# Layer 1 of a fused expert kernel: remainders in one run of row tiles, and no sums carried from one two pairs to the next

## The chip, the cores and the metric

The kernel runs on one core of a Trainium2 chip. Its time is the device time of one launch in microseconds. Besides that there is a profile of one execution, with a page of summary tables and a trace of every instruction on TensorE (PE, with its weight loads PEld), VectorE (DVE), ScalarE (ACT), GpSimd (POOL) and the DMA queues (SP is the queue of SyncE). Times in the trace count from the start of the span.

## The reference, cut to what matters

Two blocks follow each other: a recurrent attention cell (mLSTM) over 4 batches, 8 heads and 768 positions, and a mixture of 8 experts to which each of the 3072 rows is sent by a hash of its token number. The change concerns the second block and the passage to it.

```python
# attention: y (B, H, S, 40), one state update per position   ... cut ...
x = attn_out.transpose(0, 2, 1, 3).reshape(3072, 320)

expert_idx = token_ids * 2654435761 % 8
for e in range(8):
    mask = expert_idx == e
    xe = x[mask]                          # about 384 rows, 320 columns
    h = np.maximum(xe @ w1[e], 0.0)       # w1[e]: 320 x 1024   (layer 1)
    out[mask] = h @ w2[e]                 # w2[e]: 1024 x 320   (layer 2)
```

All of it is float32.

## The kernel before

The rows of an expert are gathered into 416 columns (384 and a remainder of 32), turned so that the 320 features lie along partitions: two blocks of 128 (`xT[:, 0]`, `xT[:, 1]`) and a block of 64 features, which is present twice, in partitions 0 to 63 (`lo`) and 64 to 127 (`up`). Layer 1 makes eight blocks of 128 hidden features. Expert 0 uses the plain `layer1`. Experts 1 to 7 use `layer1_pairs`: the two blocks of 128 features, two neighbouring blocks of hidden features and two halves of the columns (`c0`, `c1`, 208 each) form a product of 2x2 blocks, done with seven block products in place of eight by a scheme of sums of the Strassen kind. `wsums` holds the four sums of weights (made by POOL), `xsums` the four sums of x (made by DVE). The 64 features left over, the remainder, are added by matmuls of half height: `lo` and `up` are row tiles of PE which run at the same time and write to different PSUM banks. Each `both` is one block product for two pairs of hidden blocks, two float32 matmuls, which are four instructions in the trace. Two passes (`q`) make the eight hidden blocks.

```python
def sums_of_x(xT):
    b = [[xT[:, k, c * CH : (c + 1) * CH] for c in range(2)] for k in range(3)]
    ...                                   # t1, t2, t3, t4: four DVE sums
    nc.vector.tensor_tensor(dx[P // 2 :], b[2][0][P // 2 :], b[2][1][P // 2 :], op=ALU.subtract)
    return t1, t2, t3, t4, dx

def both(q, dst, x, y, start, stop):
    for i in range(2):
        nc.tensor.matmul(dst[:, i, :], lhsT=x(2 * q + i), rhs=y, ...)

def last(dst1, x1, dst2, x2, q, stop2):   # the remainder: two row tiles side by side
    for i in range(2):
        for d, r, x in ((dst1, lo, x1), (dst2, up, x2)):
            nc.tensor.matmul(d[:, i, :], lhsT=w1c[r, 2 * q + i, :], rhs=x, start=False, ...)

prev = None
for q in range(NQ + 1):                   # NQ = 2
    cur = None
    if q < NQ:
        A, B, Y = (PSUM banks)
        p1, u2, v = (SBUF tiles, bufs=2, 2, 1)
        cur = q, B, Y, p1, u2
        both(q, A, blk(0, 0), xT[:, 0, c0], True, True)
        nc.scalar.copy(p1[:], A[:])                                        # L1067
        both(q, B, of(s2), t2[:], True, True)
        nc.vector.tensor_tensor(u2[:], B[:], p1[:], op=ALU.add)            # L1069
        both(q, Y, of(s3), t3[:], True, False)
        between(2 * q)
    if prev:                              # second half of the pairs before
        pq, pB, pY, pp1, pu2 = prev
        both(pq, pY, blk(1, 1), t4[:], False, False)
        both(pq, pB, of(s4), xT[:, 1, c1], False, False)
    if cur and prev:
        both(q, B, of(s1), t1[:], False, True)
        nc.vector.tensor_tensor(v[:], B[:], p1[:], op=ALU.add)             # L1078
    if cur:
        last(A, xT[lo, 2, c0], Y, xT[up, 2, c1], q, True)
    if prev:
        last(pB, xT[lo, 2, c1], pY, dx[up], pq, True)
    if cur and not prev:
        both(q, B, of(s1), t1[:], False, True)
        nc.vector.tensor_tensor(v[:], B[:], p1[:], op=ALU.add)             # L1085
    if cur:
        nc.vector.tensor_tensor(hv[:, 1, ..., c1], Y[:], v[:], op=ALU.add) # L1087
    if prev:
        h0, h1 = (hv[:, i, ...] for i in range(2))
        nc.vector.tensor_tensor(h1[:, :, c0], pY[:], pu2[:], op=ALU.add)   # L1090
        nc.scalar.activation(h1, h1, AF.Relu)                              # L1091
        nc.vector.tensor_tensor(h0[:, :, c1], pB[:], pp1[:], op=ALU.add)   # L1092
        nc.scalar.activation(h0[:, :, c1], h0[:, :, c1], AF.Relu)          # L1093
    if cur:
        both(q, A, blk(1, 0), xT[:, 1, c0], False, True)
        nc.scalar.activation(hv[:, 0, ..., c0], A[:], AF.Relu)             # L1096
        between(2 * q + 1)
    prev = cur
```

`between` takes the next of the following expert's `turns`: three tiles of 128 rows and a remainder. A turn is three transposes on PE and a copy out of PSUM (tile 0 and 2 on DVE, tile 1 and the remainder on ACT). Layer 2 (`layer2_pair`) begins with one plain product and makes the others from sums in the same way; it calls `after(j)` at three points. In the loop over the experts:

```python
def one(fp):
    if ahead and (e > 0 or fp != 0 or len(ahead) < 4):
        ahead.pop(0)()
def after(j):
    if j == (e == 0) and e + 1 < E:
        xss[e + 1] = sums_of_x(xTs[e + 1])
    one(j)
    ...
```

The passage from the attention block to expert 0: the last rows are gathered, transposed and copied (L904); `rows_by_table` adds the last 256 rows by a matmul with a table of ones; `spin0(n)` issues n idle products of 416 columns (L890); DVE adds both parts (L911). Then `sums_of_w2` of expert 0 (four POOL sums, L1105) and `fetch(1)`, the gathers of expert 1's rows, follow on POOL in this order.

Of the kernel before, what the change touches and what calls it, by code (L numbers as in the profile page):

```python
# [17 lines left out]
P = 128  # L18
# [4 lines left out]
def kernel(  # L23
# [105 lines left out]
    with tc.tile_pool(name="gates", bufs=1) as gp, \  # L129
# [757 lines left out]
        def spin0(n):  # L887
            idle = ps.tile([P, CAP], F32, name="idle", tag="tr", bufs=4)
            for _ in range(n):
                nc.tensor.matmul(idle[:], lhsT=ident[:], rhs=W[0][0][:, 0, :CAP], start=True, stop=True)  # L890
# [6 lines left out]
        for i, j in enumerate((NJ, *range(NJ))):  # L897
            n = RM if j == NJ else P
            tp = ps.tile([P, DB, P], F32, name="tp0", tag="tr", bufs=4)
            for db in range(2):  # L900
                nc.tensor.transpose(tp[:, db, :n], xg0[:n, j, db * P : (db + 1) * P], ident[:n, :n])  # L901
            nc.scalar.copy(xg0[:n, j, Dm:], xg0[:n, j, 2 * P : Dm])
            nc.tensor.transpose(tp[:, 2, :n], xg0[:n, j, 2 * P :], ident[:n, :n])
            nc.scalar.copy(xT0[:, :, j * P : j * P + n], tp[:, :, :n])  # L904
            if i < DB:
                rows_by_table(1, i)
            if i == DB - 1:
                spin0(1)
        spin0(2)
        for db in range(DB):  # L910
            nc.vector.tensor_tensor(xT0[:, db, :], xT0[:, db, :], om[db][:, :CAP], op=ALU.add)  # L911

# [102 lines left out]
    def sums_of_x(xT):  # L1015

        b = [[xT[:, k, c * CH : (c + 1) * CH] for c in range(2)] for k in range(3)]
        t1, t2, t3, t4, dx = (xp.tile([P, CH], F32, name=f"xs{i}", bufs=1) for i in range(1, 6))
        nc.vector.tensor_tensor(t1[:], b[0][1], b[0][0], op=ALU.subtract)
        nc.vector.tensor_tensor(t2[:], b[1][1], t1[:], op=ALU.subtract)  # L1020
        nc.vector.tensor_tensor(t3[:], b[1][1], b[0][1], op=ALU.subtract)
        nc.vector.tensor_tensor(dx[P // 2 :], b[2][0][P // 2 :], b[2][1][P // 2 :], op=ALU.subtract)
        nc.vector.tensor_tensor(t4[:], b[1][0], t2[:], op=ALU.subtract)
        return t1, t2, t3, t4, dx

    def layer1_pairs(w, wsums, xT, xsums, h, between):

        w1t, w1c, _ = w  # L1030
        s1, s2, s3, s4 = wsums
        t1, t2, t3, t4, dx = xsums
        lo, up = slice(0, P // 2), slice(P // 2, P)
        c0, c1 = slice(0, CH), slice(CH, CAP)
        hv = h.rearrange("p (x i) c -> p i x c", i=2)

        def both(q, dst, x, y, start, stop):
            for i in range(2):
                nc.tensor.matmul(  # L1039
                    dst[:, i, :], lhsT=x(2 * q + i), rhs=y, start=(start and i == 0), stop=stop,  # L1040
                    skip_group_check=True,
                )

        def blk(k, i):
            return lambda fp: w1t[:, k, (2 * fp + i) * P : (2 * fp + i + 1) * P]

        def of(s):
            return lambda fp: s[:, fp]

        def last(dst1, x1, dst2, x2, q, stop2):  # L1050
            for i in range(2):
                for d, r, x in ((dst1, lo, x1), (dst2, up, x2)):
                    nc.tensor.matmul(
                        d[:, i, :], lhsT=w1c[r, 2 * q + i, :], rhs=x, start=False, stop=(r == lo or stop2),
                        skip_group_check=True,
                    )

        NQ = FB // 4
        prev = None
        for q in range(NQ + 1):  # L1060
            cur = None
            if q < NQ:
                A, B, Y = (mps.tile([P, 2, CH], F32, name=f"m{i}", tag="bank") for i in "aby")
                p1, u2, v = (xp.tile([P, 2, CH], F32, name=f"l{i}", bufs=2 - i // 2) for i in range(3))
                cur = q, B, Y, p1, u2
                both(q, A, blk(0, 0), xT[:, 0, c0], True, True)
                nc.scalar.copy(p1[:], A[:])  # L1067
                both(q, B, of(s2), t2[:], True, True)
                nc.vector.tensor_tensor(u2[:], B[:], p1[:], op=ALU.add)  # L1069
                both(q, Y, of(s3), t3[:], True, False)  # L1070
                between(2 * q)
            if prev:
                pq, pB, pY, pp1, pu2 = prev
                both(pq, pY, blk(1, 1), t4[:], False, False)
                both(pq, pB, of(s4), xT[:, 1, c1], False, False)
            if cur and prev:
                both(q, B, of(s1), t1[:], False, True)
                nc.vector.tensor_tensor(v[:], B[:], p1[:], op=ALU.add)  # L1078
            if cur:
                last(A, xT[lo, 2, c0], Y, xT[up, 2, c1], q, True)  # L1080
            if prev:
                last(pB, xT[lo, 2, c1], pY, dx[up], pq, True)
            if cur and not prev:
                both(q, B, of(s1), t1[:], False, True)
                nc.vector.tensor_tensor(v[:], B[:], p1[:], op=ALU.add)  # L1085
            if cur:
                nc.vector.tensor_tensor(hv[:, 1, 2 * q : 2 * q + 2, c1], Y[:], v[:], op=ALU.add)  # L1087
            if prev:
                h0, h1 = (hv[:, i, 2 * pq : 2 * pq + 2, :] for i in range(2))
                nc.vector.tensor_tensor(h1[:, :, c0], pY[:], pu2[:], op=ALU.add)  # L1090
                nc.scalar.activation(h1, h1, AF.Relu)  # L1091
                nc.vector.tensor_tensor(h0[:, :, c1], pB[:], pp1[:], op=ALU.add)  # L1092
                nc.scalar.activation(h0[:, :, c1], h0[:, :, c1], AF.Relu)  # L1093
            if cur:
                both(q, A, blk(1, 0), xT[:, 1, c0], False, True)
                nc.scalar.activation(hv[:, 0, 2 * q : 2 * q + 2, c0], A[:], AF.Relu)  # L1096
                between(2 * q + 1)
            prev = cur

    def sums_of_w2(w2t):  # L1100

# [64 lines left out]
    with tc.manual_schedule():  # L1166
        xgs, xTs, remT, hrem = {}, {0: xT0}, {}, {}

        def fetch(e):
            if e % EG == 0 or e == 1:  # L1170
                xgs[-1 - e // EG] = xp.tile([P, DB * P], F32, name="xr")
            xgs[e] = xp.tile([P, NJ, DB * P], F32, name="xg", bufs=3)
            for j in range(NJ):
                gather(xgs[e][:, j, :Dm], cols_of(g_idx, e * NJ)(j))
            if e % EG == 0 or e == 1:
                gather(xgs[-1 - e // EG][:, :Dm], cols_of(g_idx, NR + e // EG)(0))
# [16 lines left out]
        def rest(g):  # L1193
# [6 lines left out]
                    )  # L1200
            scatter(zp, cols_of(s_idx, NR + g)(0), True)

        sums = sums_of_w2(W[0][2])
        fetch(1)


        for piece in weight_slices(1):
# [2 lines left out]
        for e in range(E):  # L1210
            g, i = e // EG, e % EG
            if e + 2 < E:
                fetch(e + 2)
            if e > 0:
                sums = sums_of_w2(W[e][2])
            h = xp.tile([P, FB, CAP], F32, name="h", bufs=1)
            if i == 0:
                hrem[g] = xp.tile([P, EG, FB, RM], F32, name="hrem")
            ahead = turns(e + 1) if e + 1 < E else []

            def one(fp):
                if ahead and (e > 0 or fp != 0 or len(ahead) < 4):
                    ahead.pop(0)()

            def after(j):
                if j == (e == 0) and e + 1 < E:
                    xss[e + 1] = sums_of_x(xTs[e + 1])
                one(j)
                if j == 0 and i == EG - 1:
                    rest(g)  # L1230

            if e + 1 < E:
                wnext, pieces = sums_of_w1(W[e + 1][0])
            if e == 0:
                layer1(W[e], xTs[e], h, CAP, one)
            else:
                layer1_pairs(W[e], wsums, xTs[e], xss[e], h, one)
            for piece in pieces:
                piece()
            pieces = []  # L1240
            nc.scalar.copy(hrem[g][:, i], h[:, :, NM:])
            layer2_pair(W[e], sums, h, cols_of(s_idx, e * NJ), after)
            wsums = wnext

            if e + 2 < E:
                for j in range(NJ):
                    nc.scalar.copy(xgs[e + 2][:, j, Dm:], xgs[e + 2][:, j, 2 * P : Dm])
                if (e + 2) % EG == 0:
                    xr = xgs[-1 - (e + 2) // EG]
                    nc.scalar.copy(xr[:, Dm:], xr[:, 2 * P : Dm])  # L1250
            if e + 3 < E:
                slices = weight_slices(e + 3)
                if e == 0:
                    slices[1:1] = weight_slices(2)
                for piece in slices:
                    piece()
# [51 lines left out]
```

## Time and profile before

| what | value |
|---|---|
| time, median of 3 | 405.84 us (404.99 to 406.05) |
| span of the profiled execution | 402.9 us |
| granted TensorE clock, mean | 0.983 |
| DVE busy | 221.3 us (55%) |
| ACT busy | 148.8 us (37%) |
| POOL busy | 201.3 us (50%) |
| `ma`, `mb`, `my` full-height matmuls, 128x208, each | 339 to 346 ns |
| row tiles of the remainder, 64x208, each | 336 ns |

[...]matmuls that follow each other overlap. What a matmul costs is read from the distance between two starts. The engine lines of the timeline give the start, the duration, the engine, the line of the program, what is written and read, and in brackets how long the engine sat idle before and which instruction ended it. The attention block fills about the first 155 us, expert 0 begins at 167.8, expert 1 at 196.9, and the last product of expert 7 ends at about 394.

### The profile page before, as it was taken

To read this page: it belongs to the slowest core of one execution; us is meant where nothing else is said; L and a number is where in the kernel's file an instruction comes from. 1 tells how busy PE (TensorE), PEld (TensorE's weight loads), DVE (VectorE), ACT (ScalarE), POOL (GpSimd) and SP (SyncE) were. 2 spreads that over 40 slices of the span, in tenths; PEclk is the share of its full clock that TensorE was granted. 3 is DMA by queue.
4 is the path that set the end of the run, shared out by engine and by line. 5 is a ranking of instruction groups with operands and counts; after the bars stand their busy time and mean duration, and the time that the engine had idled before them with its cause. 6 is when DMAs were issued, how large, how long until landed. Compare 5 with 4: busy or idle time off the path is not lost. (4 is left out here: it accounts for less than half of the span.)

```text
span 402.9 us, 8802 instructions
## 1 busy us (share of the span) xinstructions
PE 378.4 (94%) x3397; PEld 311.6 (77%) x3397; DVE 221.3 (55%) x537; ACT 148.8 (37%) x290; POOL 201.3 (50%) x253
## 2 busy tenths in 40 slices
PE   8789979999999997899999999999999999999991
PEld 8668868877877774457898978978979989889780
DVE  8657557778797984133447356462455463453500
ACT  6335785575676541222132231141131141321310
POOL 6653103324535634881295593871692874807011
PEclk9969999999999999999999999999999999999996
DMA  7588846977767513835938245244244200000000
GB/s 150 111 174 190 205 107 152 242 197 176 151 149 182 132 65 126 285 83 164 333 129 272 75 130 171 83 130 152 83 142 142 78 16 33 2 15 34 0 17 36
DMA packets 96616, 51.53 MB, mean 128 GB/s; under 512 B 68455, under 2 KB 90604, under 8 KB 96572
## 3 DMA queue, kind: packets, MB, share of 16 engines
q1 hardware_dynamic: 90956, 39.29, 37.8%
q0 software_dynamic: 2528, 8.24, 6.2%
q10 hardware_dynamic: 3088, 3.41, 2.8%
q8 instruction: 28, 0.46, 0.5%
q14 instruction: 16, 0.13, 0.1%
HBM read 42.02 MB, written 8.65 MB: 126 GB/s over the span
## 5 line engine op out<-in xcount | busy, mean ns | idle before, releaser
L929 POOL DMA_INDIRECT out_dram<-zo,s_idx x26 | 26.9, 1035 | 91.5 <-DVE zo L1159 53.2
L476 POOL TENSOR_TENSOR x<-x,den 128x320 f32<-128x320 f32 x21 | 15.1, 723 | 48.8 <-DVE den L474 27.4
L387 DVE TENSOR_TENSOR w<-sp,w 128x512 f32<-128x512 f32 x48 | 30.9, 686 | 12.6 <-PE sp L379 12.0
L1121 PE MATMUL zp<-w2t,h 128*128 128x320 f32 x128 | 36.5, 438 | 0.0
L379 PE MATMUL sp<-qT,kT 64*128 64x128 f32 x384 | 29.4, 291 | 2.7 <-ACT qT L316 1.5
L379 PEld LDWEIGHTS sp<-qT,kT 64*128 64x128 f32 x384 | 24.6, 193 | 9.3 <-issue 4.6
L1121 PEld LDWEIGHTS zp<-w2t,h 128*128 128x128 f32 x128 | 23.2, 190 | 11.1 <-issue 1.8
L1091 ACT ACTIVATE h<-h 128x832 f32<-128x832 f32 x14 | 12.6, 898 | 47.6 <-DVE h L1090 47.6
L342 ACT ACTIVATE w<-ab 128x512 f32<-128x512 f32 x48 | 26.6, 608 | 7.5 <-PE ab L338 7.5
L1131 PE MATMUL zp<-t,s 128*128 128x160 f32 x192 | 27.5, 299 | 0.6 <-DVE s L1116 0.6
L437 PE MATMUL ht<-w,v 128*64 128x128 f32 x384 | 27.1, 285 | 0.0
L1131 PEld LDWEIGHTS zp<-t,s 128*128 128x128 f32 x192 | 26.5, 190 | 0.8 <-POOL ws L1013 0.8
L1105 POOL TENSOR_TENSOR t<-w2t 128x640 f32<-128x640 f32 x16 | 24.8, 1548 | 1.7 <-PE tp L901 1.6
L1105 POOL TENSOR_TENSOR t<-w2t,t 128x640 f32<-128x640 f32 x16 | 24.7, 1545 | 0.6
L1039 PE MATMUL mb<-xs,ws 128*128 128x208 f32 x112 | 25.0, 346 | 0.0
L1039 PE MATMUL ma<-xT,w1t 128*128 128x208 f32 x112 | 24.8, 346 | 0.0
L437 PEld LDWEIGHTS ht<-w,v 128*64 128x64 f32 x384 | 21.2, 140 | 4.0 <-issue 3.3
L919 POOL DMA_INDIRECT xg<-x_rows,g_idx x21 | 20.3, 966 | 6.2 <-issue 5.8
L449 ACT COPY hB<-ht 128x512 f32<-128x512 f32 x20 | 11.7, 587 | 30.8 <-PE ht L437 29.2
L1039 PEld LDWEIGHTS mb<-xs,ws 128*128 128x128 f32 x112 | 19.6, 190 | 1.8 <-issue 1.8
L458 PE MATMUL xo<-ident,hB 128*128 128x128 f32 x96 | 16.3, 298 | 4.3 <-ACT hB L449 2.2
L1039 PEld LDWEIGHTS ma<-xT,w1t 128*128 128x128 f32 x112 | 18.9, 190 | 1.8 <-issue 1.8
(261 smaller groups left out, 888.7 us busy)
## 6 DMA issues: line engine op xcount, KB each, us to landing
w2t<-in_moe_w_dram SPq DMA_DIRECT2D x28, 320.0 KB
w1t<-in_moe_w_dram SPq DMA_DIRECT2D x28, 256.0 KB
k<-in_k_dram SPq DMA_DIRECT2D x24, 160.0 KB
v<-in_v_dram SPq DMA_DIRECT2D x24, 160.0 KB
x_rows<-x SPq DMA_DIRECT2D x22, 160.0 KB
ql<-in_q_dram SPq DMA_DIRECT2D x6, 480.0 KB
og<-in_o_gate_dram SPq DMA_DIRECT2D x6, 480.0 KB
w1c<-in_moe_w_dram SPq DMA_DIRECT2D x14, 128.0 KB
```

Source lines behind the costliest of these rows:

```text
L342: nc.scalar.activation(w[:, hf], ab[:], AF.Exp)
L379: nc.tensor.matmul(sp[hf][:, j, :], lhsT=d["kT"][r, j, :], rhs=q_of(s)[r, j, :], start=True, stop=True,)
L387: nc.vector.tensor_tensor(d["w"][:, hf], d["sp"][hf][:], d["w"][:, hf], op=ALU.mult)
L437: nc.tensor.matmul(place(j, hf), lhsT=d["v"][:, 2 * j + hf, :], rhs=d["w"][:, hf, j, :], start=(c == 0 and j0 == 0), stop=True, skip_group ...
L458: nc.tensor.transpose(xo[:, hf, i, :], src[:, hf, i, :], ident[:])
L476: eng.tensor_tensor(xv, xv, den[:].to_broadcast([P, 2, PR, D]), op=ALU.mult)
L919: nc.gpsimd.indirect_dma_start(out=xg, out_offset=None, in_=x_d[:, :], in_offset=bass.IndirectOffsetOnAxis(ap=idx, axis=0),)
L929: ins = nc.gpsimd.indirect_dma_start(out=out[:, :], out_offset=bass.IndirectOffsetOnAxis(ap=idx, axis=0), in_=zo[:], in_offset=None, bound ...
L1039: nc.tensor.matmul(dst[:, i, :], lhsT=x(2 * q + i), rhs=y, start=(start and i == 0), stop=stop, skip_group_check=True,)
L1105: nc.gpsimd.tensor_tensor(d[:], x, y[:] if y in (t1, t2) else y, op=ALU.subtract)
L1121: nc.tensor.matmul(zp[:], lhsT=h[:, fb, 2 * P : 3 * P], rhs=w2t[:, fb, :], start=(fb == 0), stop=(fb == FB - 1),)
L1131: nc.tensor.matmul(dst, lhsT=x[:, i], rhs=y[:, i], start=(start and i == 0), stop=(i == FB // 2 - 1), skip_group_check=True,)
```

## The change

Layer 1 of experts 1 to 7 is put into another order. Each pass over two pairs is complete in itself: it takes five PSUM banks in place of three, so that both halves of the remainder can start sums of their own (`B2`, `Y2`), all eight half-height products of a pass stand in one run, and nothing is carried into the next pass. It needs one DVE sum more (`u3`) and one less (`dx`). In expert 0 the first turn is made one place earlier, so that all four lie in layer 1, the sums of x move with it, the gathers of expert 1 are issued ahead of the sums of w2, and of three idle products before expert 0 one is left. It is for having fewer switches between full-height and half-height products on PE, and for a simpler flow with shorter-lived buffers.

```diff
-            if i == DB - 1:
-                spin0(1)
-        spin0(2)
+        spin0(1)
 ... sums_of_x: dx and its sum removed ...
-        def last(dst1, x1, dst2, x2, q, stop2):
-            for i in range(2):
-                for d, r, x in ((dst1, lo, x1), (dst2, up, x2)):
-                    nc.tensor.matmul(d[:, i, :], lhsT=w1c[r, 2 * q + i, :], rhs=x, start=False, ...)
-        ... the loop shown above ...
+        def last(pairs, q):
+            for lo_, up_ in pairs:
+                for i in range(2):
+                    for (d, x, start, stop), r in ((lo_, lo), (up_, up)):
+                        nc.tensor.matmul(d[:, i, :], lhsT=w1c[r, 2 * q + i, :], rhs=xT[r, 2, x],
+                            start=(start and i == 0), stop=stop, skip_group_check=True)
+
+        for q in range(FB // 4):
+            A, B, Y, B2, Y2 = (mps.tile([P, 2, CH], F32, name=f"m{i}", tag="bank") for i in range(5))
+            p1, u2, u3, v = (xp.tile([P, 2, CH], F32, name=f"l{i}", bufs=1) for i in range(4))
+            h0, h1 = (hv[:, i, 2 * q : 2 * q + 2, :] for i in range(2))
+            both(q, A, blk(0, 0), xT[:, 0, c0], True, True)
+            nc.scalar.copy(p1[:], A[:])
+            both(q, B, of(s2), t2[:], True, True)
+            nc.vector.tensor_tensor(u2[:], B[:], p1[:], op=ALU.add)
+            both(q, Y, of(s3), t3[:], True, True)
+            nc.vector.tensor_tensor(u3[:], Y[:], u2[:], op=ALU.add)
+            between(2 * q)
+            both(q, B, of(s1), t1[:], False, True)
+            nc.vector.tensor_tensor(v[:], B[:], p1[:], op=ALU.add)
+            last([((A, c0, False, False), (Y2, c0, True, False)),
+                  ((B2, c1, True, False), (Y, c1, False, True))], q)
+            nc.vector.tensor_tensor(h1[:, :, c1], Y[:], v[:], op=ALU.add)
+            both(q, A, blk(1, 0), xT[:, 1, c0], False, True)
+            nc.scalar.activation(h0[:, :, c0], A[:], AF.Relu)
+            both(q, B2, of(s4), xT[:, 1, c1], False, True)
+            nc.vector.tensor_tensor(h0[:, :, c1], B2[:], v[:], op=ALU.add)
+            nc.scalar.activation(h0[:, :, c1], h0[:, :, c1], AF.Relu)
+            both(q, Y2, blk(1, 1), t4[:], False, True)
+            nc.vector.tensor_tensor(h1[:, :, c0], Y2[:], u3[:], op=ALU.add)
+            nc.scalar.activation(h1, h1, AF.Relu)
+            between(2 * q + 1)
 ...
+        fetch(1)
         sums = sums_of_w2(W[0][2])
-        fetch(1)
 ...
-            def one(fp):
-                if ahead and (e > 0 or fp != 0 or len(ahead) < 4):
+            def one(_):
+                if ahead:
                     ahead.pop(0)()
             def after(j):
-                if j == (e == 0) and e + 1 < E:
+                if j == 0 and e + 1 < E:
                     xss[e + 1] = sums_of_x(xTs[e + 1])
```

More of the change, by code (lines that the diff above doesn't have):

```diff
@@ L1017, in sums_of_x @@
         b = [[xT[:, k, c * CH : (c + 1) * CH] for c in range(2)] for k in range(3)]
-        t1, t2, t3, t4, dx = (xp.tile([P, CH], F32, name=f"xs{i}", bufs=1) for i in range(1, 6))
+        t1, t2, t3, t4 = (xp.tile([P, CH], F32, name=f"xs{i}", bufs=1) for i in range(1, 5))
         nc.vector.tensor_tensor(t1[:], b[0][1], b[0][0], op=ALU.subtract)
@@ L1021, in sums_of_x @@
         nc.vector.tensor_tensor(t3[:], b[1][1], b[0][1], op=ALU.subtract)
-        nc.vector.tensor_tensor(dx[P // 2 :], b[2][0][P // 2 :], b[2][1][P // 2 :], op=ALU.subtract)
         nc.vector.tensor_tensor(t4[:], b[1][0], t2[:], op=ALU.subtract)
-        return t1, t2, t3, t4, dx
+        return t1, t2, t3, t4
     def layer1_pairs(w, wsums, xT, xsums, h, between):
@@ L1031, in layer1_pairs @@
         s1, s2, s3, s4 = wsums
-        t1, t2, t3, t4, dx = xsums
+        t1, t2, t3, t4 = xsums
         lo, up = slice(0, P // 2), slice(P // 2, P)
@@ L1048, in of @@
             return lambda fp: s[:, fp]
-        def last(dst1, x1, dst2, x2, q, stop2):
-            for i in range(2):
-                for d, r, x in ((dst1, lo, x1), (dst2, up, x2)):
[L1053 to L1098, printed above, removed]
@@ new lines, in last @@
+        def last(pairs, q):
+            for lo_, up_ in pairs:
+                for i in range(2):
+                    for (d, x, start, stop), r in ((lo_, lo), (up_, up)):
+                        nc.tensor.matmul(
+                            d[:, i, :], lhsT=w1c[r, 2 * q + i, :], rhs=xT[r, 2, x], start=(start and i == 0), stop=stop,
+                            skip_group_check=True,
+                        )
+        for q in range(FB // 4):
[11 more added lines that the diff above has]
+            nc.vector.tensor_tensor(v[:], B[:], p1[:], op=ALU.add)
+            last([((A, c0, False, False), (Y2, c0, True, False)), ((B2, c1, True, False), (Y, c1, False, True))], q)
+            nc.vector.tensor_tensor(h1[:, :, c1], Y[:], v[:], op=ALU.add)
[8 more added lines that the diff above has]
+            between(2 * q + 1)
```

## The prediction

> **What bounds the kernel now.** I read the page first, for the busiest engine:
>
> ```profile
> PE 378.4 (94%) x3397; PEld 311.6 (77%) x3397; DVE 221.3 (55%) x537; ACT 148.8 (37%) x290; POOL 201.3 (50%) x253
> ```
>
> TensorE (PE) carries 94% of the span, so a change is worth what it takes from PE's instructions or from PE's gaps. The table of stretches, one stretch per expert from one first product of layer 1 to the next, shows how dense PE is (columns: stretch, its length, then busy time and count for PE, weight loads, DVE, ACT and POOL, granted clock, DMA share, GB/s):
>
> ```profile
> 196.90:223.68 26.78, 26.78 (x172) 23.92 (x171) 13.51 (x26) 6.99 (x17) 17.72 (x14) 1.00 0.64 202
> 223.68:251.32 27.64, 27.00 (x171) 23.93 (x170) 14.67 (x26) 7.13 (x18) 19.10 (x15) 1.00 0.43 137
> ...
> 309.85:336.62 26.77, 26.77 (x171) 23.91 (x170) 13.60 (x26) 6.99 (x17) 17.71 (x14) 1.00 0.11 37
> ```
>
> An undisturbed expert takes 26.78 us, all of it with PE busy, at a granted clock of 1.00. The one that begins at 223.68 loses 27.64 - 26.78 = 0.86 us (two others are longer because they hold the product of the collected remainders). So in the seven experts that use the pairwise layer 1 there is hardly any idle time to recover: what can be saved is what PE spends inside its own stream. The timeline of PE alone shows where that is, at the middle run of row tiles of expert 1:
>
> ```profile
> 206.02 0.87 PE L1039 MATMUL mb<-xs,ws 128*128 128x208 f32 x4
> 206.82 0.44 PE L1053 MATMUL ma<-xT,w1c 64*128 64x208 f32 x1
> ...
> 207.10 0.34 PE L1053 MATMUL ma<-xT,w1c 64*128 64x208 f32 x1
> ...
> 208.15 0.34 PE L1053 MATMUL mb<-xT,w1c 64*128 64x208 f32 x1
> ...
> 208.43 0.97 PE L1039 MATMUL ma<-xT,w1t 128*128 128x208 f32 x4
> 209.23 0.87 PE L1039 MATMUL my<-xs,w1t 128*128 128x208 f32 x4
> ```
>
> One full-height product of four instructions takes 0.70 us elsewhere in the stream (from 209.23 to the next one at 209.94), 0.174 us an instruction. Here the last product before the run starts at 206.02 and should be through at 206.72, but the first row tile starts at 206.82; the second follows after 0.28 instead of 0.174; the last, at 208.15, should be through at 208.33, but the full-height product starts at 208.43 and needs 0.80 instead of 0.70. Four times 0.10: a run costs 0.40 us beyond its own work, going in and coming out, whatever its length. Layer 1 of one expert has three runs.
>
> The whole timeline of the same expert gives the durations of the short chains on DVE and ACT:
>
> ```profile
> 197.80 0.51 ACT L1067 COPY l<-ma 128x416 f32<-128x416 f32 x1 [3.16 <-PE ma L1039]
> ...
> 198.58 0.59 DVE L1069 TENSOR_TENSOR l<-mb,l 128x416 f32<-128x416 f32 x1 [0.92 <-PE mb L1039]
> ...
> 202.46 0.47 ACT L947 COPY xT<-tp 128x384 f32<-128x384 f32 x1
> ...
> 211.75 0.59 DVE L1090 TENSOR_TENSOR h<-my,l 128x416 f32<-128x416 f32 x1 [2.12 <-PE my L1053]
> ...
> 212.38 0.90 ACT L1091 ACTIVATE h<-h 128x832 f32<-128x832 f32 x1 [1.31 <-DVE h L1090]
> ...
> 213.19 0.53 ACT L1093 ACTIVATE h<-h 128x416 f32<-128x416 f32 x1
> ```
>
> The copy p1 (L1067) starts 0.90 after the first product of A (196.90). The sum u2 (L1069) starts 0.98 after the first matmul of B's product (197.60), takes 0.59, and ends at 199.17. A DVE sum is followed by its relu 0.04 later (212.34 to 212.38); the long relu holds ACT for 0.81 (212.38 to 213.19), the copy of a turned tile (L947) for about 0.37, p1 for 0.51.
>
> Last, the first expert, which uses another layer 1, from the same view of the transition:
>
> ```profile
> 165.38 1.56 PE L890 MATMUL idle<-w1t,ident 128*128 128x416 f32 x4
> ...
> 165.58 0.48 ACT L904 COPY both<-tp 128x384 f32<-128x384 f32 x1 [1.10 <-PE tp L903]
> ...
> 166.09 1.08 DVE L911 TENSOR_TENSOR both<-both,sp 128x416 f32<-128x416 f32 x2 [5.26 <-ACT both L904]
> ...
> 167.82 3.03 PE L968 MATMUL mh<-both,w1t 128*128 128x416 f32 x8 [0.88 <-DVE both L911]
> ...
> 193.53 0.38 DVE L1023 TENSOR_TENSOR xs<-xT,xs 128x208 f32<-128x208 f32 x1
> 193.83 0.32 DVE L1151 TENSOR_TENSOR u<-zp,u 128x160 f32<-128x160 f32 x1
> ...
> 194.18 0.33 DVE L1152 TENSOR_TENSOR zo<-zp,u 128x160 f32<-128x160 f32 x1
> ...
> 194.65 1.32 PE L1131 MATMUL zp<-t,h 128*128 128x160 f32 x8 [0.77 <-DVE zo L1152]
> ```
>
> The adds L911 wait for the copy L904, not for the idle matmuls (L890), but PE issues two of those ahead of the transposes which that copy waits for. And PE stands for 0.77 us at 194.65, because the sums of x (L1023 and four before it) sit on DVE ahead of the adds (L1151, L1152) that this product waits for.
>
> **What the Trainium skill says.** "TensorEngine Tiling (Array Packing)", Key Properties: "Changing tiling mode (not just tile) drains the TensorE". The trace agrees, 0.40 us a run. The same page, Gotcha 1: different row tiles cannot access one PSUM bank at the same time; in both kernels the two halves of each pair go to different banks, and the pairs in the trace start within 0.01 us of each other. "SBUF — State Buffer", Who interferes with whom: a DVE instruction with two SBUF inputs contends with a GpSimd instruction that reads SBUF, one with a single SBUF input doesn't. In the trace a sum of two SBUF tiles (L1115) takes 0.69 us alone and 1.64 beside a GpSimd sum; the sums that the change adds take one input from PSUM, and 0.59 throughout. "TensorE: Matmul & The Clock Gate", What's actually happening: the clock halves after an idle window of about 3.4 us. The gap which a removed idle product leaves is an estimated 1.6 us, below that; no run here shows where the threshold lies.
>
> **The change, part by part.** (1) Runs of row tiles. Per expert, 14 full-height products and 8 pairs of row tiles stay as they are, 14 x 0.704 + 16 x 0.174 = 12.6 us. The runs fall from three to two. Seven experts: 7 x 0.40 = 2.8 us saved.
>
> (2) The two pairs after each other. Before, the second half of one pair's work was mixed into the next pair, which gave DVE and ACT time. Now each pair must finish, and PE needs u2 read before it may add s1*t1 to B. I lay the second pair out from the start s of the product Y2, the last of the first pair. PE: Y2 0.70, transposes of the second tile 0.33, A 0.70, B 0.70, Y 0.70, transposes of the third tile 0.33: the product s1*t1 could start at s + 3.48. The other path: the sum h1 starts 0.98 after Y2 does and ends at s + 1.57; relu from s + 1.61 holds ACT to 2.42; the second tile's copy stands in front of p1, to 2.79; p1 ends at 3.30; u2 runs from 3.33 to 3.92; PE sees it about 0.12 later (167.67 to 167.79 for L911 and the load that waits for it), at s + 4.04. PE waits 4.04 - 3.48 = 0.56 us, say 0.57. That is a new wait, in each of the six experts with turns: 3.4 us. In the last expert there are no turns: PE could start at s + 2.82, the other path without the tile's copy gives s + 3.67, a wait of 0.85; and in its first pair u2 is visible at 2.27 + 0.12 = 2.39 after A's start while PE is there at 3 x 0.704 = 2.11, another 0.28. With turns the first pair just fits: 2.39 against 2.44. Together 3.4 + 1.1 = 4.5 us given back.
>
> (3) DVE and ACT work. One more sum of 0.59 per two pairs (u3), one of 0.37 less per expert (dx). DVE is at 55% and gains nothing on the path from this. Five PSUM banks for each two pairs out of eight: going round the banks, each new tile takes one whose last reader finished more than 1 us before, by the same layout, so no wait there.
>
> (4) First expert. One idle product of 416 columns less before the last transposes: two instructions of 0.35, so 0.69 us earlier for L904, the adds, and PE's first product. The other removed one lay beside the adds and is worth nothing. The fourth turn moves from layer 2 into layer 1: same PE time. The sums of x move from after the second point of layer 2 to the first, ahead of which DVE is idle for microseconds: the 0.77 us at 194.65 go. The first tile's transposes now come after the first eight matmuls, about 167.1 + 2.8 = 169.9. Its gather is issued earlier, since it stands before the sums of w2 on GpSimd, but the last store of x_rows has to land first: by the waits of the SP queue (4.1 us after the issue at 160.9) about 165.0. The gather takes 1 us on GpSimd; for its landing I estimate 2 to 3 more, from the store issued at 151.4 whose landing the first gather awaited until 154.4: 168 to 169. I charge 0.2. Sum: -0.69 - 0.77 + 0.2 = -1.3.
>
> Sum of all: -2.8 + 4.5 - 1.3 = +0.4 us, so 406.2 from 405.84.
>
> **Rivals.** First: the mode switches are all there is, and p1 and u2 come in time. For it: PE has no wait in layer 1 today, and DVE and ACT are half idle. Against it: their idle time lies elsewhere; the chain from h1 through relu and copy to u2 is in order on ACT. It would give -2.8 - 1.3 = -4.1, 401.7. Second: the new wait is larger, because a DVE sum starts late. For it: in expert 1 the sum u2 of the second pair started at 204.93, about 1 us after its inputs, and at 232.96 a copy did; today that costs nothing, in the new order every such microsecond on h1 or u2 lands on PE. With one such delay in every other expert: +3 more, 409.5. Third: the first tile's gather comes late and PE stands inside the first layer 1, up to 2 us: 408. Fourth: with the three idle products cut to one, the clock falls at the start of expert 0; ten us at half speed would be +5. The gap is short, so I give it little.
>
> **Range and chances.** The saved runs are sure to 0.3 us, since every run in the trace shows the same 0.10 steps. The new wait carries the spread: 0.57 is the difference of two sums of about 4 us, each good to 0.1 or 0.2, times seven. The second rival stretches the upper side, the first the lower. So 406.2, and 403.2 to 408.6 for 8 in 10. Two per cent is 8.1 us; nothing above reaches it alone, so within 2% has 0.97, faster 0.015, slower 0.015.
>
> **What would show it.** Right: two runs of eight row tiles per expert with the same 0.10 steps; a gap of some 0.6 us on PE ahead of the product s1*t1 of the second two pairs, put down to the DVE sum u2, in experts 1 to 6, and a larger one in 7; an undisturbed expert of 26.78 - 0.40 + 0.57 = 26.95 us; the first matmul of expert 0 about 0.7 earlier; no gap before the third group of layer 2 of expert 0. Wrong: an expert of 26.4 us (no new wait: step 2 falls), one over 27.3 (a longer chain than laid out), or PE waiting for a gather in expert 0.

## The result, and the profile after

| | time, median (us) | ratio to before, 95% interval |
|---|---|---|
| before | 405.94 (404.99 to 406.95) | |
| after | 412.62 (410.49 to 413.31) | 1.0152 (1.0114 to 1.0191) |

The change makes the kernel 1.5% slower; 406.2 us was predicted, in a range of 403.2 to 408.6. The profiled execution is one of 410.49 us, with a span of 408.5 against 402.9: 5.6 of the loss can be read in its trace. The other executions took one to three us more; what they lost beyond this one no trace shows.

From the page of the changed kernel, PE's busy time and the row of the granted clock in 40 slices, tenths of full speed:

```profile
PE 378.9 (93%) x3393; PEld 312.0 (76%) x3393; DVE 225.4 (55%) x544; ACT 149.7 (37%) x290; POOL 200.5 (49%) x253
...
PEclk9969999999999999789999999999999999999998
```

PE's busy time has grown by 0.5 us only, and its share has fallen from 94 to 93%. The clock shows a 7 and an 8 in the 17th and 18th slice (163 to 184 us), where the row of before has nines. That is the passage to expert 0. Its timeline (start, duration, engine, line; line numbers have moved by two: L909 are the adds, L966 the first products of expert 0, L942 the small copy inside a turn):

```profile
164.86 0.94 POOL L917 DMA_INDIRECT xg<-x_rows,g_idx  x1 [4.08 <-PE ht L881]
165.16 0.25 ACT L902 COPY both<-both 128x64 f32<-128x64 f32 x1 [0.64 <-DMA both<-x_rows,g_first]
...
165.63 0.86 PE L890 MATMUL idle<-w1t,ident 128*128 128x416 f32 x2
...
165.83 0.48 ACT L904 COPY both<-tp 128x384 f32<-128x384 f32 x1 [0.42 <-PE tp L903]
...
168.82 0.20 DVE L942 COPY xg<-xg 128x64 f32<-128x64 f32 x1 [8.87 <-DMA xg<-x_rows,g_idx]
168.93 1.08 DVE L909 TENSOR_TENSOR both<-both,sp 128x416 f32<-128x416 f32 x2
...
170.66 5.61 PE L966 MATMUL mh<-both,w1t 128*128 128x416 f32 x8 [4.16 <-DVE both L909]
```

The last copy L904 ends at 166.31. In the kernel before, the adds followed it within 0.03 us. Here DVE first does L942, the copy of 64 columns of expert 1's first gathered tile. The source has the adds first, but the compiled program has this copy ahead of them on DVE, and it can't start before the gather that POOL issued at 164.86 has landed, at 168.82. (Why the compiler put it there, no run shows.) The adds start at 168.93 and PE's first product at 170.66, 4.83 us after the start of the last L904; before it was 167.82 - 165.58 = 2.24. So 2.59 us are a hold of the adds. The first eight matmul instructions then take 5.61 us against 3.03. The table of stretches (length, busy times, then the granted clock, DMA share, GB/s) says why:

```profile
166.00:170.66 4.66, 0.50 (x3) 0.04 (x1) 1.69 (x4) 0.31 (x1) 3.93 (x4) 0.83 0.84 260
170.66:176.10 5.44, 5.44 (x8) 2.72 (x9) 0.00 (x0) 0.00 (x0) 5.21 (x5) 0.52 0.38 142
```

During the hold PE was busy for 0.50 of 4.66 us. In steps of 0.1 us the granted clock is 1.00 up to 169.0, some 2.5 us after the end of the idle product (165.63 + 0.86), and 0.50 from there to 175.9. That gives the means of 0.83 and 0.52 in these two lines. The eight instructions take another 2.58 us for it.

The experts with the pairwise layer 1, in the same table; expert 1, from its first product to the next expert's:

```profile
201.33:228.21 26.88, 26.64 (x172) 24.02 (x170) 14.19 (x27) 7.12 (x17) 17.43 (x14) 1.00 0.70 223
```

It takes 26.88 us against 26.78, and now has 0.24 us in which PE is not busy. From the first product of expert 1 to the end it is 408.5 - 201.33 = 207.2 against 402.9 - 196.90 = 206.0. The loss is 1.2 us here, and 201.33 - 196.90 = 4.4 us up to there. In the timeline of expert 1 the one run of row tiles of the first pass looks as it should:

```profile
203.76 0.87 PE L1035 MATMUL m<-xs,ws 128*128 128x208 f32 x4
...
204.56 1.68 PE L1051 MATMUL m<-xT,w1c 64*128 64x208 f32 x16
...
206.17 0.97 PE L1035 MATMUL m<-xT,w1t 128*128 128x208 f32 x4
```

The product ahead of it starts at 203.76 and would be through at 204.46; the run starts at 204.56; sixteen row tiles, eight pairs, take 8 x 0.174 and two losses of 0.10, to 206.17; the product after it takes 0.80 instead of 0.70 (the next one starts at 206.97). It costs 0.40 us beyond its work, as before, and there are two in an expert, not three. What takes the saving back stands in the second pass:

```profile
209.21 0.90 ACT L1078 ACTIVATE h<-h 128x832 f32<-128x832 f32 x1 [0.15 <-DVE h L1077]
...
210.37 0.51 ACT L1061 COPY l<-m 128x416 f32<-128x416 f32 x1
...
210.82 0.38 PE L940 MATMUL tp<-ident,xg 128*128 128x128 f32 x2
...
210.91 0.59 DVE L1063 TENSOR_TENSOR l<-m,l 128x416 f32<-128x416 f32 x1 [1.74 <-ACT l L1061]
...
211.55 0.97 PE L1035 MATMUL m<-xs,ws 128*128 128x208 f32 x4 [0.24 <-DVE l L1063]
...
212.45 1.68 PE L1051 MATMUL m<-xT,w1c 64*128 64x208 f32 x16
```

L1078 is the long relu of the first two pairs, L1061 is p1, L1063 is u2; in the line left out ACT copies the turned tile. ACT goes through relu, tile and p1 one after the other; p1 is not finished until 210.88, u2 ends at 211.50, and the product s1*t1 starts at 211.55. The transposes before it had started at 210.82 and take 0.33 of PE's stream: PE was ready at 211.15. That is a wait of 0.40 us (the bracket says 0.24, since it counts from the end of the last transpose). The product then takes 0.90 up to the run at 212.45, where it took 0.80 in the first pass (203.76 to 204.56). So the stop costs 0.50 us, and 26.78 - 0.40 + 0.50 = 26.88 is the expert's time.

### The profile page after: what moved, and what is told of

It reads as the page before. It is cut to its first block, busy times and chain, and to the rows that moved or that the text cites. A ratio compares the mean times of both kernels' runs of the same rounds, so it can differ in the third digit from the quotient of the medians.

```text
span 408.5 us, 8829 instructions
## 1 busy us (share of the span) xinstructions
PE 378.9 (93%) x3393; PEld 312.0 (76%) x3393; DVE 225.4 (55%) x544; ACT 149.7 (37%) x290; POOL 200.5 (49%) x253
## 5 line engine op out<-in xcount | busy, mean ns | idle before, releaser
L1035 PE MATMUL m<-xs,ws 128*128 128x208 f32 x168 | 35.0, 344 | 2.0 <-DVE l L1063 2.0
L1035 PEld LDWEIGHTS m<-xs,ws 128*128 128x128 f32 x168 | 29.0, 190 | 4.1 <-DVE l L1063 4.1
L1102 PEld LDWEIGHTS zp<-w2t,h 128*128 128x128 f32 x128 | 24.1, 190 | 8.9
L1072 ACT ACTIVATE h<-m 128x416 f32<-128x416 f32 x14 | 7.2, 517 | 60.9 <-PE m L1035 60.9
L1035 PE MATMUL m<-xT,w1t 128*128 128x208 f32 x112 | 25.7, 352 | 0.0
L1051 PE MATMUL m<-xT,w1c 64*128 64x208 f32 x224 | 23.5, 349 | 0.0
L1051 PEld LDWEIGHTS m<-xT,w1c 64*128 64x128 f32 x224 | 19.0, 186 | 3.5 <-issue 3.5
```

The lines of the kernel that those rows point to most:

```text
L1035: nc.tensor.matmul(dst[:, i, :], lhsT=x(2 * q + i), rhs=y, start=(start and i == 0), stop=stop, skip_group_check=True,)
L1102: nc.tensor.matmul(zp[:], lhsT=h[:, fb, 2 * P : 3 * P], rhs=w2t[:, fb, :], start=(fb == 0), stop=(fb == FB - 1),)
```

## The experiments

Theory 1: the loss is the hold of the adds by one small copy in DVE's order, and the clock that falls while PE waits for it; the pairwise layer 1 costs about 1 us. Theory 2: the clock falls because two of three idle products were taken away. Theory 3: the new waits in the pairwise layer 1 carry the loss. Each run was timed against the kernel before on the same chip; of its profile the distance from the start of the last L904 to the first product of expert 0 and to that of expert 1 is compared, since the attention block ends up to 2 us earlier or later from one execution to the next.

| run | median (us) | before beside it | ratio, 95% interval | L904 to expert 0 | first 8 instructions | L904 to expert 1 |
|---|---|---|---|---|---|---|
| before | 405.94 | | | 2.24 | 3.03 | 31.32 |
| after | 412.62 | 405.94 | 1.0152 (1.0114 to 1.0191) | 4.83 | 5.61 | 35.50 |
| 1 turn late | 406.12 | 405.76 | 1.0009 (0.9991 to 1.0027) | 2.25 | 3.03 | 31.19 |
| 2 copy on ACT | 406.68 | 405.76 | 1.0031 (1.0012 to 1.0050) | 2.24 | 3.03 | 31.81 |
| 3 seven idle products | 408.75 | 405.76 | 1.0105 (1.0063 to 1.0147) | 4.96 | 3.03 | 33.04 |
| 4 gather late | 413.79 | 405.76 | 1.0222 (1.0189 to 1.0256) | 8.26 | 5.18 | 38.49 |
| 5 relu late | 402.83 | 405.54 | 0.9936 (0.9913 to 0.9959) | 2.24 | 4.68 | 32.45 |
| 6 all turns in layer 1 | 404.39 | 405.54 | 0.9966 (0.9946 to 0.9985) | 2.24 | 4.68 | 32.73 |
| 7 runs cut in two | 411.12 | 405.54 | 1.0143 (1.0114 to 1.0171) | 2.23 | 4.73 | 32.50 |
| 8 pairs alone | 405.91 | 405.54 | 1.0019 (1.0000 to 1.0038) | 2.25 | 3.03 | 30.81 |
| 9 relu late, three idle | 403.29 | 405.79 | 0.9949 (0.9930 to 0.9967) | 2.24 | 3.03 | 31.32 |
| 10 idle products alone | 406.09 | 405.79 | 0.9998 (0.9982 to 1.0014) | 2.24 | 3.03 | 31.31 |

### 1. The first turn late again

```diff
 # on the changed kernel
-            def one(_):
-                if ahead:
+            def one(fp):
+                if ahead and (e > 0 or fp != 0 or len(ahead) < 4):
                     ahead.pop(0)()
-                if j == 0 and e + 1 < E:
+                if j == (e == 0) and e + 1 < E:
```

> The changed kernel, with the first turn of expert 0 back at its old place (after the second pair of hidden blocks) and the sums of x back at the second point of layer 2. Theory 1 (the small DVE copy of the gathered tile stands ahead of the three adds in the compiled order and holds them until the gather has landed, and the clock falls while PE waits): adds and first product follow the last copy L904 at once, about 2.6 us of gap and 2.6 us of half clock go, 0.8 us for the sums of x come back: about 408 us. Theory 2 (one idle product in place of three lets the clock fall by itself): half clock in expert 0 stays, about 411. Theory 3 (the new waits in the pairwise layer 1 carry the loss): 412 to 413, as the changed kernel.

406.12 us. The timeline of this kernel at the passage:

```profile
168.59 1.08 DVE L909 TENSOR_TENSOR both<-both,sp 128x416 f32<-128x416 f32 x2 [6.79 <-ACT both L904]
...
170.32 3.03 PE L966 MATMUL mh<-both,w1t 128*128 128x416 f32 x8 [1.58 <-DVE both L909]
```

The adds are released by the last copy L904 (168.07 + 0.48), the first product follows, at full clock. Each beside its own kernel before, the loss falls from 6.7 us to 0.4: this one edit takes back 6.3 us by the medians (5.8 by the ratios), two more than expected. The profiles show 35.50 - 31.19 = 4.3 of them; the rest no trace shows. Theory 1 had the mechanism right; theories 2 and 3 fall as main causes.

### 2. The early turn stays, its small copy goes to ACT

```diff
-            nc.vector.tensor_copy(xg[:, Dm:], xg[:, 2 * P : Dm])
+            nc.scalar.copy(xg[:, Dm:], xg[:, 2 * P : Dm])
```

> The changed kernel with only this different: the small copy of a gathered tile's last 64 columns runs on ACT, whose compiled order has it after the last L904, and not on DVE. The early turn stays. Theory 1: the adds no longer wait, the gather is hidden behind the first eight matmuls, about 407.3 us. Theory 2: the clock falls as before, 410 to 411. Theory 3: unchanged, 412.6.

406.68 us. In its timeline the copy still waits for its gather, but the adds no longer wait behind it:

```profile
168.14 3.03 PE L966 MATMUL mh<-both,w1t 128*128 128x416 f32 x8 [1.58 <-DVE both L909]
...
169.34 0.24 ACT L942 COPY xg<-xg 128x64 f32<-128x64 f32 x1 [2.96 <-DMA xg<-x_rows,g_idx]
...
176.83 0.33 PE L943 MATMUL tp<-ident,xg 128*128 128x128 f32 x1 [0.52 <-ACT xg L942]
```

PE is at its first product at 168.14 while the gather lands at 169.34, well ahead of the transposes. So an early turn does not cost the 6 us; its place in DVE's queue does. It gains nothing over the late turn either: now the last transposes of two later turns wait for the copy on ACT behind a relu, 0.52 us each (the last line is one of them).

### 3. PE kept busy during the hold

```diff
-        spin0(1)
+        spin0(7)
```

> The changed kernel with seven idle products in place of one ahead of the adds, so that PE is busy while DVE waits for the gather. Theory 1: the wait of the adds stays, the first product starts at the same place as in the changed kernel, and runs at full clock: 2.6 us less, about 410. Theory 2: all is regained, about 407. Theory 3: unchanged, 412.6.

408.75 us. The hold is there, the slow clock is not:

```profile
169.11 0.20 DVE L942 COPY xg<-xg 128x64 f32<-128x64 f32 x1 [9.27 <-DMA xg<-x_rows,g_idx]
...
171.07 3.03 PE L966 MATMUL mh<-both,w1t 128*128 128x416 f32 x8
```

The first product comes 4.96 us after the last L904, as in the changed kernel, but its eight instructions take 3.03: PE spent the hold on idle products. By the last column this is worth 35.50 - 33.04 = 2.46 us. The medians give 3.9, more than the 2.6 expected, from five executions between 407.61 and 412.00. In the profiles the split is: the hold 2.6, the clock 2.6.

### 4. The gather later

```diff
-        fetch(1)
         sums = sums_of_w2(W[0][2])
+        fetch(1)
```

> The changed kernel with the gathers of expert 1 behind the four sums of w2 on POOL again, as before the change. Theory 1: the gather is issued at about 167.3 and not 164.9, so the adds and the first product of expert 0 start some 2.4 us later, and the cold stretch is not shorter: 415 to 416 us. Theories 2 and 3: the order of the gathers does not matter, 412.6.

413.79 us, less than expected. The timeline:

```profile
171.71 0.22 DVE L942 COPY xg<-xg 128x64 f32<-128x64 f32 x1 [12.17 <-DMA xg<-x_rows,g_idx]
...
173.57 5.18 PE L966 MATMUL mh<-both,w1t 128*128 128x416 f32 x8 [7.59 <-DVE both L909]
```

The adds move with the gather, as theory 1 demands. Seen from the last L904 it is issued 2.3 us later (166.68 - 165.31 against 164.86 - 165.83) and takes 1.1 longer to land, and the first product comes 3.4 us later, 8.26 in place of 4.83. By the two ratios the time grew by 0.7%, 2.8 us, by the two medians only by 1.2; the profiles, with 3.0 us up to expert 1, stand nearer to the ratios.

### 5. The long relu behind p1

```diff
 # on the first experiment
+        late = []
         for q in range(FB // 4):
 ...
             nc.scalar.copy(p1[:], A[:])
+            while late:
+                late.pop()()
             both(q, B, of(s2), t2[:], True, True)
 ...
-            nc.scalar.activation(h1, h1, AF.Relu)
+            late.append(lambda h1=h1: nc.scalar.activation(h1, h1, AF.Relu))
             between(2 * q + 1)
+        while late:
+            late.pop()()
```

> The first experiment (turn late), with the long relu of h1 of the first two pairs put behind the copy p1 of the second two on ACT. If the wait ahead of s1*t1 in the second two pairs (0.40 us in an expert with turns, more in the last) comes from relu and tile copy standing in front of p1 on ACT, then p1 starts 0.9 after its product, u2 is read in time, and about 6 x 0.40 + 0.8 = 3.2 us go: 402.9 us, an expert of 26.5 us in place of 26.88. If the wait is due to DVE being late for other reasons (its extra sum u3, or POOL's sums), it stays, and the time is 406.

402.83 us, as expected, and faster than the kernel before by 0.64% (0.41 to 0.87). The second pass of expert 1 in its timeline, lines as above (L1062 p1, L1081 the relu, L1066 u2):

```profile
206.82 0.51 ACT L1062 COPY l<-m 128x416 f32<-128x416 f32 x1 [0.25 <-PE m L1035]
207.23 0.90 ACT L1081 ACTIVATE h<-h 128x832 f32<-128x832 f32 x1
...
207.54 0.59 DVE L1066 TENSOR_TENSOR l<-m,l 128x416 f32<-128x416 f32 x1 [1.21 <-PE m L1035]
...
208.30 0.87 PE L1035 MATMUL m<-xs,ws 128*128 128x208 f32 x4
```

p1 comes first, u2 ends at 208.13, PE starts s1*t1 at 208.30 without a wait. The stretch of expert 1 in the first experiment:

```profile
199.26:226.16 26.90, 26.65 (x172) 24.04 (x171) 14.19 (x27) 7.12 (x17) 17.43 (x14) 1.00 0.63 209
```

And here, experts 1 and 6:

```profile
198.48:225.00 26.52, 26.52 (x172) 24.03 (x170) 14.76 (x27) 7.21 (x17) 17.43 (x14) 1.00 0.62 194
...
336.98:363.36 26.38, 26.38 (x172) 24.00 (x171) 13.20 (x27) 6.79 (x14) 14.15 (x11) 1.00 0.05 19
```

26.52 us, all of it busy: 0.38 less than in the first experiment, 0.26 less than before the change. ACT's order made the wait. Expert 6 shows what the saved run is worth, 26.78 - 26.38 = 0.40; in expert 1, 0.14 of it is lost again in layer 2 (12.07 us there, 11.93 in expert 6).

Its profile holds a surprise, in the stretch of expert 0's first products:

```profile
168.27:172.88 4.61, 4.61 (x9) 2.20 (x9) 0.00 (x0) 0.00 (x0) 4.20 (x5) 0.64 0.86 289
```

PE's gap ahead of them was 1.58 us as in the first experiment, but here the mean granted clock was 0.64, and the eight instructions took 4.68 us. By its time it is not the usual case: this execution took 404.94 us at a mean clock of 0.975 over the whole span, the five others 402.68 to 403.37 us at 0.983 to 0.989.

### 6. All turns inside layer 1 without the early one

```diff
 # on the fifth experiment
+            def one(fp):
+                if e == 0 and fp == 0:
+                    return
+                for _ in range(2 if e == 0 and fp == 3 else 1):
+                    if ahead:
+                        ahead.pop(0)()
-                if j == (e == 0) and e + 1 < E:
+                if j == 0 and e + 1 < E:
```

> The late relu, and in expert 0 no turn at the first place but two at the last, so that all turns lie in layer 1 and the sums of x stand at the first point of layer 2 as in the change. The adds are not held, the stop of 0.26 to 0.8 us in layer 2 of expert 0 goes: 402.3 us, 0.8 to 0.9% under the kernel before. If the two turns together at the last place make PE wait, as much comes back.

404.39 us: not better than the fifth. Two turns in a row make PE wait for the second one's small copy:

```profile
186.13 0.33 PE L943 MATMUL tp<-ident,xr 128*128 128x128 f32 x1 [0.53 <-DVE xr L942]
```

0.53 us are lost here, of the size of what the stop in layer 2 cost (0.77 before the change, 0.26 in the profile of the first experiment). By the last column the two differ by 0.28 us; the rest of the 1.6 between their medians is not explained. (The profile of the fifth stands 2.1 us above its median, this one 0.2, so they need not show the same kind of execution.)

### 7. Each run cut in two

```diff
 # on the first experiment
-            last([((A, c0, False, False), (Y2, c0, True, False)), ((B2, c1, True, False), (Y, c1, False, True))], q)
-            nc.vector.tensor_tensor(h1[:, :, c1], Y[:], v[:], op=ALU.add)
+            last([((A, c0, False, False), (Y2, c0, True, False))], q)
             both(q, A, blk(1, 0), xT[:, 1, c0], False, True)
             nc.scalar.activation(h0[:, :, c0], A[:], AF.Relu)
+            last([((B2, c1, True, False), (Y, c1, False, True))], q)
+            nc.vector.tensor_tensor(h1[:, :, c1], Y[:], v[:], op=ALU.add)
```

> The first experiment with the run of eight row-tile pairs of each pass cut in two by one full-height product; same matmuls, four runs per expert instead of two. If a run costs 0.40 us whatever its length: 2 x 0.40 x 7 = 5.6 us more than the first experiment, 411.7. If the saving by fewer runs was not real (the switches hidden behind other work), no more than 0.5.

411.12 us, 5.0 over the first experiment. The stretch of expert 1:

```profile
200.24:227.92 27.68, 27.44 (x172) 23.81 (x170) 13.74 (x27) 7.12 (x17) 16.93 (x14) 1.00 0.66 210
```

The same stretch of the first experiment has 26.90 us. 27.68 - 26.90 = 0.78 us for two more runs: 0.39 each, with the same matmuls. The saving is real.

### 8. The pairwise layer 1 alone

```diff
 # on the kernel before: sums_of_x and layer1_pairs of the changed kernel, nothing else
```

> The kernel before with nothing changed but the pairwise layer 1 (five banks, one run of row tiles in a pass). By the trace of the changed kernel the seven experts together lose 1.2 us: 407.0. If the pairwise layer 1 carries the loss of the changed kernel after all: 411 to 412.

405.91 us, 0.2% over before (0.00 to 0.38), and 1.1 under the expected. The first product of expert 1 in its timeline:

```profile
196.46 0.87 PE L1037 MATMUL m<-xT,w1t 128*128 128x208 f32 x4
```

From there to the end it has 403.7 - 196.46 = 207.2 us, as the changed kernel has: this part costs 1.2 us. Up to expert 1 it gains 31.32 - 30.81 = 0.51: one sum of x less stands ahead of the adds of layer 2 in expert 0, and PE stands there for 0.26 us in place of 0.77. So the core of the change is nearly neutral.

### 9. Late relu with three idle products

```diff
 # on the fifth experiment
-        spin0(1)
+        spin0(3)
```

> The kernel of the fifth experiment (late relu, turn late) with three idle products instead of one between the last transposes and the adds, 2.1 us of work beside a distance of 2.2 us, so that PE has hardly a gap before expert 0. In the profiles of three kernels with one idle product the first eight products of expert 0 took 4.7 us and not 3.0. If the short gap (1.6 us) lets the clock fall in part of the executions: always 3.0 us here, the median 0.5 to 1.5 us under the fifth experiment's, 401.5 to 402.5, with a smaller spread. If the clock fell for another reason: still 4.7 in the profile, median 402.8.

403.29 us. The gap is gone, PE goes from the idle products to the first product within 0.18 us, at full clock:

```profile
167.68 3.03 PE L966 MATMUL mh<-both,w1t 128*128 128x416 f32 x8 [0.18 <-DVE both L909]
```

But the median is not below that of the fifth experiment, nor is the spread smaller (403.08 to 405.17), so the half of the expectation that spoke of the time was wrong. The expectation took the profile of the fifth for the usual case; by their mean clocks, most executions of the fifth seem to have had no such fall.

### 10. The idle products alone

```diff
 # on the kernel before
-            if i == DB - 1:
-                spin0(1)
-        spin0(2)
+        spin0(1)
```

> The kernel before with nothing changed but the idle products, one instead of three. The step of the prediction: 0.69 us faster, 405.1. The rival: the last copy waits for its gather anyway, so nothing is gained, and where the clock falls expert 0 is 1.7 us later: 405.5 to 407, with a wider spread.

406.09 us, no difference (0.9998). The 0.69 us that the prediction wrote down for the earlier transposes would be a ratio of 0.9983, at the very edge of the interval. The trace speaks against them: without the idle product PE stands ahead of the last transposes until their gather has landed.

```profile
165.09 0.41 PE L901 MATMUL tp<-ident,both 128*128 128x128 f32 x2 [0.43 <-DMA both<-x_rows,g_first]
```

The spread, expected wider, is not (404.59 to 406.72, before 404.75 to 408.15).

## Why the prediction was wrong, by its own steps

**What bounds the kernel** held: PE is dense, and every loss found here is time in which PE waited or ran slowly.

**Step 1**, the saved runs of 0.40 us, was right: two runs per expert in the trace, 0.39 each by experiment 7. The drain that the Trainium skill states ("TensorEngine Tiling (Array Packing)", Key Properties) is paid per switch: four pairs or eight in a run cost the same.

**Step 2**, the new wait, was right in place and cause. Its length was 0.40 us where 0.57 was worked out: u2 started 3.23 us after s and not 3.33, and PE followed its end by 0.05 and not 0.12. The step left out the 0.10 us by which the product behind the wait is longer, so the stop costs 0.50. In expert 7 two waits of about 0.2 and 0.7 stand for 0.28 and 0.85. The two steps were to give +1.7 us, the seven experts lost 1.2. Experiment 5 removed the wait by ACT's order alone.

**Step 3** was right: no wait for a bank, none for the sum u3.

**Step 4** failed. It gave -1.3 us for the passage and expert 0; from the last L904 to the first product of expert 1 the profile shows 35.50 - 31.32 = +4.2. Its terms, one by one:
- "about 167.1 + 2.8 = 169.9" took the adds to come right behind L904 and the early turn to touch nothing before its transposes. That is the sentence which failed. The turn also has a copy on DVE, and I placed it by the order of the source. In the compiled program it stands ahead of the adds. The landing of the gather was estimated well, 168 to 169 against 168.82, but what waits for it is not a transposition hidden behind eight matmuls: it is every add, and with them all of expert 0. Charged 0.2, found 2.6 (experiments 1, 2 and 4).
- The gap of PE was estimated at 1.6 us; with the hold it became 4.2, and the clock fell: 2.6 more (experiment 3). The Trainium skill's idle window of about 3.4 us ("TensorE: Matmul & The Clock Gate", What's actually happening), on which the prediction leaned for the short gap, is no safe limit here. In the changed kernel the clock fell some 2.5 us after PE's last work, and in experiments 5 to 7 a gap of 1.6 us was enough, while in 1, 2 and 10 the same gap had no effect. The measurement decides. The traces of these six differ a little earlier: ahead of the last transposes PE waited 0.73, 0.89 and 1.27 us in 5 to 7, and 0.40, 0.27 and 0.43 in 1, 2 and 10. No experiment varied that wait, so it is a lead and not a cause. The fourth rival named this mechanism and gave it little, because it looked at the gap without the hold; the third rival named the late gather, but on PE.
- -0.69 for the earlier last transposes: found nothing (experiment 10). In the timeline of the changed kernel above, L902 waits for the landing of its own gather; from the first of these gathers to the last L904 it takes 10.2 us with three idle products in experiment 8 and 10.1 with one in the changed kernel, though 11.2 in the profile of before, where that copy did not wait for its gather.
- -0.77 for the stop in layer 2: found, there is no gap there in the changed kernel.

The terms 2.6 + 2.6 - 0.8 and the 1.2 of the seven experts make 5.6 us, the difference of the two profiled spans. The other 1.1 us between the medians stay open.

One sum among the rivals is off: the second rival's 3 us more would be 409.2, not 409.5. It did not come about: in all six experts with turns the profile has the stop of 0.5 us and no longer one.

## What to carry to other kernels

When a step that needs a transfer is moved earlier, each of its instructions moves, on each engine, and an in-order queue makes everything behind the first one wait for the transfer: look where it lands in the compiled order of every engine, not where it stands in the source. A saving at one end of PE's stream is kept only if the short chain on ACT and DVE still fits; here moving one relu behind the copy that PE waits for turned a ratio of 1.001 into 0.994. A wait of several us on PE can cost more than its length: after gaps of 4.2 and 7.6 us (changed kernel and experiment 4) the next eight instructions took 2.6 and 2.2 us more, because part of them ran at half clock.

## What the runs showed of the hardware that was not expected

A gather of 128 rows of 1280 bytes, issued beside the weight loads, had landed for its first reader 4.0 us after its start in the changed kernel (164.86 to 168.82, DMA share 0.84 in that stretch) and 5.0 in the fourth experiment (166.68 to 171.71). A gap of 1.6 us on PE before expert 0 was followed by a halved clock for part of the next eight instructions in three profiles (4.68, 4.68 and 4.73 us) and by full clock in three others (3.03 us). Once fallen, the granted clock stayed at 0.50 for 3.4 us in experiments 5, 6 and 7 (168.2 to 171.6 in the fifth), for 6.8 in the changed kernel (169.0 to 175.9) and for 10.2 in the fourth experiment (167.7 to 177.9): once, twice and three times 3.4 us.
